# Output projection behind the whole gate, as seven products, with y turned by a DRAM trip and VectorE's 32x32 blocks

## The chip, the cores and the metric

The kernel runs on one NeuronCore of one Trainium2 chip. The metric is the device time of one execution in microseconds (us). Times before are given for three runs; one further execution was taken by the profiler, and every row of a profile in this document is of that execution.

## What is computed

The reference is a transformer block of two layers on one sequence of S = 2048 rows with D = 640 columns, in float32. The first layer is windowed attention, the second a gated MLP whose gate mixes rows:

```python
h  = x + attention(layernorm(x), wqkv, wo)       # 32 heads, window 256
z  = gelu(layernorm(h) @ w_in)                   # F = 1728
z1, z2 = z[..., :864], layernorm(z[..., 864:])
g  = w_sp @ z2 + b_sp[:, None]                   # w_sp is 2048 x 2048
h2 = h + (z1 * g) @ w_out                        # w_out is 864 x 640
```

Below, y is z1 * g, of 2048 x 864. Matrix products run on TensorE (PE) in three terms: each operand is split into a rounded high part and a remainder (fp32r), and hi·hi, hi·lo and lo·hi are summed in PSUM. A "piece" is such a pair hi, lo.

## The kernel before

The 2048 rows are 16 tiles of 128 (P). The stages follow each other: attention; residual and layer norm; z by pairs of tiles; then the gate g in two halves of w_sp's columns. The first gate (c = 0) takes the columns that meet the first eight tiles of z2 and stores partial sums to DRAM (g_d); the second gate (c = 1) takes the others, adds g_d's rows, then b_sp, and multiplies by z1.

The gate already goes by seven products instead of eight: tiles p and p + 8 of rows form a pair, w_sp's block and z2's columns are cut into 2x2 blocks, and B11, T1, T2, B22, T3, B21, T4 are blocks, or sums and differences of blocks, whose seven products give the four results (Strassen's scheme in Winograd's form). The pieces of w_sp lie in seven places of the buffer `aw`; the raw w_sp lies in `fx`, which has two halves of 2048 columns, one for each parity of the pair; z2's pieces are `zc` (tiles `ze`, `zl`). A gate pair is 7 x 4 x 3 = 84 matmuls of 128x432. Results are gathered in `rows[0]` to `rows[3]` (432 columns to each half).

In the second gate, the output projection of a pair of tiles is done inside the gate of the next pair. `turn_y` transposes a tile of y (128x864) on PE in seven pieces into PSUM, and ACT and VectorE (DVE) split it into `y_sp`. `final` multiplies it by w_out (`project`: 7 K tiles of 128, the last with 96 rows, 3 terms, 2 halves of 320 columns: 42 matmuls of 128x320 per tile), adds h, and stores the result. `h` rows are `hr` and `rows[1]`; w_out's pieces are `wout`. After the last gate pair, tile 14 and tile 15 of this sequence (banks `out_ps` and `out_l`) are left.

The program is a list, `steps`: one entry for each product with a post (the sum that reads the product's PSUM bank), and `at(n, f)` hangs f ahead of step n. In this part of the program no order is written out by hand: the tile scheduler takes the instructions with the list as its priority, works with modelled times, and sets the order of every engine's queue, SP's (SyncE, which issues the DMAs) among them. A queue is worked off in order, so a DMA that waits holds back all that stand behind it on SP. Dependencies become semaphore waits.

PSUM banks of the gate and the projection have tags "a" and "b" with four buffers each. `split`, `plus`, `minus` and `copy` are helpers: L717 is the line of all elementwise sums and differences (on DVE unless an engine is given), L723 that of ACT's copies.

The lines below are the functions that the change touches, with their line numbers in the profile.

Of the kernel before, what the change touches and what calls it, by code (L numbers as in the profile page):

```python
# [34 lines left out]
def block_kernel(ctx, tc, x, wqk, wv, wo, w_in, wsp, bsp, w_out, out):  # L35
# [99 lines left out]
    def split(hi, lo, raw, eng=None):  # L135

        nc.scalar.activation(hi, raw, AF.Copy)  # L137
        (eng or nc.vector).tensor_tensor(out=lo, in0=raw, in1=hi.bitcast(F32), op=OP.subtract)
# [571 lines left out]
    def bank(tag, name):  # L710
        if "d" not in pools:
            psK.close()
            pools["d"] = pool(ctx, "psD", space=PSUM)
        return pools["d"].tile([P, 512], F32, tag=tag, bufs=4, name=name)

    def plus(out, a, b, op=OP.add, eng=None):
        (eng or nc.vector).tensor_tensor(out=out, in0=a, in1=b, op=op)  # L717

    def minus(out, a, b, eng=None):
        plus(out, a, b, OP.subtract, eng)  # L720
# [41 lines left out]
    def two(t):  # L762
        return t[:, 0], t[:, 1]
# [75 lines left out]
    def open_e1():  # L839
        win_stack.close()  # L840
        p = pool(win_stack, "e1")
        e1["wout"] = p.tile([P, 2, KF, D], F32R, name="wout")
        e1["y"] = p.tile([P, 2, KF, P], F32R, name="y_sp")
        e1["z1"] = [p.tile([P, FH], F32, name=f"z1_{n}") for n in range(2)]
        e1["h"] = [p.tile([P, D], F32, name="hr"), rows[1][:, :D]]

    def turn_h(i):
        ht = mem["ho"][i % 3]
# [14 lines left out]
    def at(n, f):  # L863
        later.setdefault(n, []).append(f)
# [210 lines left out]
    def gate_pair(p, c, post, extra):  # L1075
# [81 lines left out]
        def prod(m, half, start, stop, ks=range(4)):  # L1157
            if (m in (B11, T1) or m == B21 and alone) and ks[0] == 0:
                gbank[key(m, half)] = bank("b" if m == B21 else "a", f"g{c}_{p}_{half}_{m}")
            ps = gbank[key(m, half)][:, :HF]  # L1160
            for k in ks:
                if c == 1 and p == 7 and m == T4 and k == 2:
                    turn_y(NT - 2, e1["y"])
                for x, y in ((0, 0), (0, 1), (1, 0)):
                    nc.tensor.matmul(ps, w[m][x][:, k], zc[k][m][:, y], start=start and k + x + y == 0,  # L1165
                                     stop=stop and k == 3 and x == 1, skip_group_check=True)
# [27 lines left out]
                                            (plus, g11), (copy, g21))], lambda m: None)  # L1194


    y_sp2 = view(aw, 0, 2, KF, P)

    def turn_y(n, dst, tag="b"):
        y = e1["z1"][n % 2]  # L1200
        for k0, k1 in ((0, 4), (4, KF)):
            ps = bank(tag, f"yt_ps{n}_{k0}")
            for k in range(k0, k1):
                w = min(P, FH - k * P)
                nc.tensor.transpose(ps[:w, (k - k0) * P:(k - k0 + 1) * P], y[:, k * P:k * P + w], ident)
            for k0, k1, w in ((0, 4, P),) if k0 == 0 else ((4, 6, P), (6, 7, FH - 6 * P)):
                o = (k0 % 4) * P
                split(dst[:w, 0, k0:k1], dst[:w, 1, k0:k1],
                      ps[:w, o:o + (k1 - k0) * P].rearrange("p (k t) -> p k t", k=k1 - k0))

    def project(ps, js, src, middle=None):
        for k in range(KF):
            if k == 3 and middle is not None:
                middle()
            w = min(P, FH - k * P)
            for a, b in ((0, 0), (0, 1), (1, 0)):
                for j in js:
                    nc.tensor.matmul(ps[j][:, :HD], src[:w, a, k, :], e1["wout"][:w, b, k, j * HD:(j + 1) * HD],  # L1218
                                     start=(k == 0 and a + b == 0), stop=(k == KF - 1 and a == 1))

    def tile_of(n):
        return n // 2 + 8 * (n % 2)

    def load_h(n):
        nc.sync.dma_start(e1["h"][n % 2], h_d[tile_of(n)])

    def final(n, middle=None):
        ps = [bank("b", f"out_ps{n}_{j}") for j in range(2)]
        project(ps, range(2), e1["y"], middle)
        for j in range(2):  # L1230
            final_half(ps, n, j, j == 1)

    def final_half(ps, n, j, store):
        ht, c = e1["h"][n % 2], slice(j * HD, (j + 1) * HD)
        plus(ht[:, c], ps[j][:, :HD], ht[:, c])
        c = slice(0 if store == 1 else j * HD, (j + 1) * HD)
        if store:
            nc.sync.dma_start(out[tile_of(n) * P:(tile_of(n) + 1) * P, c], ht[:, c])

    gate_rows = (rows[n] for n in [0, 1] + [2, 0, 3] * 5)  # L1240

    def second_gate(p):
        i, j = 2 * p, 2 * p + 1
        gi, gj = next(gate_rows), next(gate_rows)
        n0 = len(steps)
        if p == 0:
            at(n0, open_e1)
        g = {11: gi[:, :HF], 12: gi[:, HF:], 21: gj[:, :HF], 22: gj[:, HF:]}

        def add(n):  # L1250
            def run(ps):
                plus(g[n], ps, g[n])
                side["tick"] = g[n][:, :1]
            return run

        def gated(n):
            t, c = (p + 8, j) if n > 20 else (p, i)
            z = e1["z1"][c % 2][:, HF * (n % 10 - 1):HF * (n % 10)]
            nc.vector.scalar_tensor_tensor(out=z, in0=g[n], scalar=bcol[:, t:t + 1], in1=z, op0=OP.add, op1=OP.mult)

        def load_z(n):
            nc.sync.dma_start(e1["z1"][n % 2], z1_d[tile_of(n)])

        turns = (0, 1, 2, 3) if p > 1 else (0, 4, 4, 6)

        def extra(m):
            if p:
                for x, f in zip(turns, (lambda: turn_y(i - 2, e1["y"]), lambda: final(i - 2),
                                        lambda: turn_y(i - 1, e1["y"]), lambda: final(i - 1))):
                    if x == m:  # L1270
                        f()

        at(n0 - (0 if p else 1), lambda: nc.sync.dma_start(gi, g_d[p]))
        at(n0, lambda: nc.sync.dma_start(gj, g_d[p + 8]))
        at(n0 + (1 if p else 0), lambda: load_z(i))
        at(n0 + (turns[2] + 1 if p else 0), lambda: load_z(j))
        at(n0 + 4, lambda: gated(12))
        at(n0 + (6 if p == 1 else 5), lambda: gated(22))
        at(n0 + 6, lambda: gated(11))
        at(n0 + 7, lambda: gated(21))  # L1280
        at(n0 + (9 if p == 0 else 6), lambda: load_h(i))
        at(n0 + (11 if p == 0 else 7), lambda: load_h(j))
        gate_pair(p, 1, [add(11), add(22), add(12), add(12), add(22), add(11), add(21)], extra)
        if p == 0:
            def wout_raw(k):
                if k < 3:
                    return view(fx, 2048 + k * D, D)
                return e1["h"][0] if k % 2 else rows[3][:, :D]

            def load_wout(k):  # L1290
                nc.sync.dma_start(wout_raw(k), w_out[k * P:(k + 1) * P, :])

            def put_wout(k):
                one = const.tile([P, 1], F32, tag="onew", bufs=2, name=f"onew{k}")
                nc.vector.tensor_scalar(out=one, in0=side["tick"], scalar1=1.0, scalar2=1.0, op0=OP.max, op1=OP.min)
                hi, lo = (e1["wout"][:, t, k] for t in range(2))
                nc.scalar.activation(hi, wout_raw(k), AF.Copy, scale=one)
                minus(lo, wout_raw(k), hi.bitcast(F32))

            for k, (t, u) in enumerate(((-9, 1), (-8, 2), (-7, 3), (0, 4), (2, 6), (4, 8), (6, 9))):  # L1300
                at(n0 + t, lambda k=k: load_wout(k))
                at(n0 + u, lambda k=k: put_wout(k))

    for p in range(8):
        z_pair(p, 2 * p, 2 * p + 1, win1)
# [7 lines left out]
        z2_pair(12 + p, p + 8, p + 12, p)  # L1313
    for p in range(8):
        second_gate(p)

    def run(n):
        for f in later.pop(n, []):
# [51 lines left out]
        if n > 2:  # L1370
            next(w2p, None)
    run(len(steps))
    run(len(steps) + 1)
    assert not later, sorted(later)
    n = NT - 2
    final(n, lambda: turn_y(n + 1, y_sp2, "a"))
    ps = [bank("b", f"out_l{j}") for j in range(2)]
    for j in range(2):
        project(ps, (j,), y_sp2)
        final_half(ps, n + 1, j, 2)  # L1380


# [25 lines left out]
```

## Time and profile before

| | |
|---|---|
| runs | 1109.02, 1111.28, 1111.66 us; median 1111.28 us |
| profiled execution, first to last instruction (span) | 1108.2 us |
| PE busy | 1084.3 us, 98% |
| VectorE (DVE) busy | 720.7 us, 65% |
| ScalarE (ACT) busy | 571.0 us, 52% |
| GpSimd (POOL) busy | 369.6 us, 33% |
| DMA | 187.80 MB, mean 169 GB/s |

The page gives no other time for the profiled execution than its span; the three runs lie 0.8 to 3.5 us above it, the median 3.1 us. Stages in the span: the second gate with the projections from 861.4 us to about 1090, the last two tiles to 1104.8 us, and the last stores to the end. In a row of groups, `xN` is the number of instructions, then come the sum of their busy time in us and the mean of one in ns, then the engine's idle time ahead of them. "PEld" is the loading of matmul weights, which lies beside PE's work. In a row of windows the columns are PE, PEld, DVE, ACT and POOL busy with the instructions of each, then the clock granted to PE, the share of the 16 DMA engines' time that was taken, and the GB/s moved.

### The profile page before, as it was taken

To read this page: it belongs to the slowest core of one execution; us is meant where nothing else is said; L and a number is where in the kernel's file an instruction comes from. 1 tells how busy PE (TensorE), PEld (TensorE's weight loads), DVE (VectorE), ACT (ScalarE), POOL (GpSimd) and SP (SyncE) were. 2 spreads that over 40 slices of the span, in tenths; PEclk is the share of its full clock that TensorE was granted. 3 is DMA by queue.
4 is the path that set the end of the run, shared out by engine and by line. 5 is a ranking of instruction groups with operands and counts; after the bars stand their busy time and mean duration, and the time that the engine had idled before them with its cause. 6 is when DMAs were issued, how large, how long until landed. Compare 5 with 4: busy or idle time off the path is not lost.

```text
span 1108.2 us, 27795 instructions
## 1 busy us (share of the span) xinstructions
PE 1084.3 (98%) x10667; PEld 974.4 (88%) x10667; DVE 720.7 (65%) x2043; ACT 571.0 (52%) x1215; POOL 369.6 (33%) x524
## 2 busy tenths in 40 slices
PE   9999999999999999989999999999999999999998
PEld 7998877668888877788899999999999999999998
DVE  6541212879999998677567478676637985566543
ACT  4333433249999999567776567433326531122210
POOL 3114444457777778512100055256422000000000
PEclk9999999999999999999999999999999999999999
DMA  7212565565666654678755421447593663444321
GB/s 261 74 35 96 166 221 179 196 210 181 214 204 214 215 177 120 193 254 281 242 188 193 151 80 39 165 154 233 190 339 113 204 215 114 129 132 150 100 91 65
DMA packets 88501, 187.80 MB, mean 169 GB/s; under 512 B 11648, under 2 KB 48144, under 8 KB 84448
## 3 DMA queue, kind: packets, MB, share of 16 engines
q1 hardware_dynamic: 83728, 172.08, 47.8%
q0 software_dynamic: 2336, 8.70, 2.2%
q10 hardware_dynamic: 2304, 5.24, 1.2%
q8 instruction: 84, 1.38, 0.5%
q14 instruction: 49, 0.40, 0.1%
HBM read 121.66 MB, written 65.52 MB: 169 GB/s over the span
## 4 chain that ended last, share of the span: by engine, by line
PE 78%; DMA 8%; DVE 3%; issue 3%; POOL 3%; ACT 3%; SPq 2%; ACTq 0%; POOLq 0%; DVEq 0%
PE g L1165 20%; PE zb L968 9%; PE out_ps L1218 8%; PE pv L435 6%; PE bank L341 5%; PE bank L407 5%; PE zx L916 3%; PE zv L916 2%; PE qk L525 2%; PE qk L526 2%; PE qk L527 2%; DMA qk_d<-sg 2%; PE zy L916 2%; SPq L320 1%; PE zw L916 1%
## 5 line engine op out<-in xcount | busy, mean ns | idle before, releaser
L410 ACT ACTIVATE pt<-bank 128x384 f32<-128x384 f32 (+2 forms) x512 | 200.8, 496 | 10.4 <-PE bank L407 5.7
L1165 PE MATMUL g<-zl,aw 128*128 128x432 f32 x768 | 169.7, 359 | 0.0
L353 DVE CUSTOM_DVE_ANT_0 junk<-bank,strip 128x288 bf16<-128x288 f32 x392 | 157.7, 454 | 4.3 <-PE bank L341 3.0
L723 ACT ACTIVATE aw<-fx 128x512 fp32r<-128x512 f32 (+2 forms) x147 | 84.9, 592 | 141.1 <-PE g L1165 101.9
L1165 PEld LDWEIGHTS g<-zl,aw 128*128 128x128 f32 x768 | 143.5, 188 | 6.1
L1165 PE MATMUL g<-ze,aw 128*128 128x432 f32 x576 | 131.9, 359 | 1.1 <-DVE row L717 1.1
L435 PE MATMUL pv<-pt,v_sb 128*32 128x192 f32 (+3 forms) x1984 | 127.3, 323 | 3.8 <-POOL pt L415 1.3
L717 DVE TENSOR_TENSOR aw<-fx,aw 128x512 fp32r<-128x512 f32 (+2 forms) x146 | 99.4, 690 | 28.6 <-ACT aw L723 23.5
L1165 PEld LDWEIGHTS g<-ze,aw 128*128 128x128 f32 x576 | 107.1, 188 | 6.2 <-DVE row L717 1.8
L407 PE MATMUL bank<-slot 123*32 123x288 bf16 (+5 forms) x1536 | 106.1, 282 | 1.0 <-ACT pt L410 0.4
L412 POOL TENSOR_SCALAR_AFFINE_SELECT pt<-pt 128x512 f32<-128x512 f32 x128 | 82.9, 648 | 43.6 <-ACT pt L410 42.4
L1218 PE MATMUL out_ps<-wout,y_sp 128*128 128x320 f32 (+1 forms) x630 | 96.4, 309 | 0.4 <-ACT y_sp L137 0.4
L968 PE MATMUL zb<-win,aw 128*128 128x432 f32 x480 | 95.0, 359 | 0.5 <-ACT aw L723 0.5
L1218 PEld LDWEIGHTS out_ps<-wout,y_sp 128*128 128x128 f32 (+1 forms) x630 | 94.2, 188 | 1.0 <-ACT y_sp L137 0.7
L968 PEld LDWEIGHTS zb<-win,aw 128*128 128x128 f32 x480 | 90.1, 188 | 5.0 <-ACT aw L723 0.9
L341 PE MATMUL bank<-slot 120*32 120x288 bf16 (+2 forms) x1264 | 89.8, 285 | 1.1 <-DVE mcol L353 1.0
L541 DVE TENSOR_TENSOR rest<-qk,sg 128x512 f32<-128x512 f32 x40 | 27.7, 692 | 86.1 <-ACT sg L539 86.1
L415 POOL TENSOR_SCALAR_AFFINE_SELECT pt<-pt 128x512 f32<-128x512 f32 x112 | 74.6, 666 | 0.0
L717 DVE TENSOR_TENSOR row<-g,row 128x432 f32<-128x432 f32 x80 | 48.2, 603 | 33.8 <-PE g L1165 30.3
L544 POOL TENSOR_TENSOR sg<-rest,sg 128x512 bf16<-128x512 f32 x40 | 46.6, 1166 | 69.2 <-ACT sg L543 60.2
L435 PEld LDWEIGHTS pv<-pt,v_sb 128*32 128x32 f32 x1984 | 59.5, 110 | 10.3 <-POOL pt L415 3.2
L407 PEld LDWEIGHTS <-slot 123*32 123x32 bf16 x1536 | 52.6, 96 | 16.2 <-issue 5.0
(216 smaller groups left out, 2195.1 us busy)
## 6 DMA issues: line engine op xcount, KB each, us to landing
fx<-wsp_in SPq DMA_DIRECT2D x30, 512.0 KB
slot<-qk_d SPq DMA_DIRECT2D x72, 200.0 KB
qk_d<-sg SPq DMA_DIRECT2D x32, 384.0 KB
slot<-qk_d SPq DMA_DIRECT2D x72, 160.0 KB
fx<-hn_d SPq DMA_DIRECT2D x32, 320.0 KB
o_d<-ot SPq DMA_DIRECT2D x64, 128.0 KB
z_d<-row SPq DMA_DIRECT2D x18, 432.0 KB
g_d<-row SPq DMA_DIRECT2D x16, 432.0 KB
```

The source lines that it names most:

```text
L341: nc.tensor.matmul(ps[32 * j:32 * j + 32, :n], part(st, half, 120, 0, hh, q0, 32), part(st, half, 120, 1, hh, lo + skip * j, n), start=Tru ...
L353: nc.vector.tensor_tensor_reduce(out=junk[:, :n], in0=ps[:, :n], in1=keep, scale=1.0, scalar=NEG, op0=OP.add, op1=OP.max, accum_out=m_cols ...
L407: nc.tensor.matmul(ps[32 * i:32 * i + 32, b:e], part(st, half, 123, 1, hh, k0, 32), part(st, half, 123, 0, hh, kb * P + b, e - b), start=T ...
L410: nc.scalar.activation(pt[:, hh, :n], ps[:, :n], AF.Exp, scale=SCALE)
L412: nc.gpsimd.affine_select(out=pt[:, :, :P], in_=pt[:, :, :P], pattern=[[0, 4], [1, P]], base=0, channel_multiplier=-1, compare_op=OP.is_ge ...
L435: nc.tensor.matmul(ps[32 * hh:32 * hh + 32, a - 512 * c:b - 512 * c], v_sb[:, kb, v0:v0 + 32], pt[:, hh, a - kb * P:b - kb * P], start=fir ...
L717: (eng or nc.vector).tensor_tensor(out=out, in0=a, in1=b, op=op)
L723: nc.scalar.activation(out, a, AF.Copy)
L916: nc.tensor.matmul(ps, a[x], b[:, y], start=start and m + x + y == 0, stop=stop and m == n - 1 and x == 1, skip_group_check=True)
L968: nc.tensor.matmul(b[0][:, :HF], a[t][:, x, kk], win2[0][:, y, kk, h * HF:(h + 1) * HF], start=kk + x + y == 0, stop=kk == KD - 1 and x == 1)
L1165: nc.tensor.matmul(ps, w[m][x][:, k], zc[k][m][:, y], start=start and k + x + y == 0, stop=stop and k == 3 and x == 1, skip_group_check=True)
L1218: nc.tensor.matmul(ps[j][:, :HD], src[:w, a, k, :], e1["wout"][:w, b, k, j * HD:(j + 1) * HD], start=(k == 0 and a + b == 0), stop=(k == K ...
```

## The change

The second gate no longer contains the projection. Its eight pairs follow each other, 84 matmuls each, and y's tiles are stored to a DRAM buffer. Then come eight `out_pair`s, which are one product of 2x2 blocks each: rows are tiles n and n + 8, columns are w_out's two halves of 320, and K is cut into two halves of 3 tiles. Seven products of 3 K tiles (63 matmuls) do the work of 6 K tiles, and K tile 6 (96 rows) is multiplied in the plain way for the four results (12 matmuls). That is 75 matmuls of 128x320 per pair, 600 in all, in place of 672.

y gets its transposed form so: `store_y` writes a tile to `y_d` by four DMAs, each of 32x27 runs of 32 floats, such that block columns come to lie as wanted; `load_y` reads a tile back by two DMAs, one of 96 partitions x 896 whose DRAM side is 3 x 32 x 896, one of 32 x 768; and `turn_y` is now one VectorE transposition of 32x32 blocks of 128x896. w_out's rows are put in an order to match, outside of the kernel. The sums of y's blocks (`y_prep`) are made on GpSimd, their high parts on ACT, their low parts on VectorE and two of eight on GpSimd. w_out's pieces go into z2's places `zc` as these come free in the last gate pair; its sums are made on GpSimd in gate pairs 2 to 5. Each out pair has nine sums into h's rows of 128x320 by VectorE, and one row of h and one of the result per tile, as before.

The core of the diff:

```diff
+    y_d = dram.tile([NT, 32, 4 * KF * P], F32, name="y_d")
...
-                if c == 1 and p == 7 and m == T4 and k == 2:
-                    turn_y(NT - 2, e1["y"])
...
-    def turn_y(n, dst, tag="b"):
...
-    def project(ps, js, src, middle=None):
...
-    def final(n, middle=None):
...
+        def store_y(t):
+            dst = y_d[(i, j)[t]].rearrange("j (c a i) -> a j c i", a=4, i=32)
+            for a in range(4):
+                nc.sync.dma_start(dst[a, :, :FH // 32],
+                                  y(t)[32 * a:32 * a + 32, :FH].rearrange("j (c i) -> j c i", i=32))
...
+    def y_block(n, t):
+        return view(fx, (n + 1) % 2 * 2048 + t * KF * P, KF * P)
+
+    def load_y(n, t):
+        y, src = y_block(n, t), y_d[n + 8 * t].rearrange("j (b c) -> b j c", b=4)
+        nc.sync.dma_start(y[:96], src[:3])
+        nc.sync.dma_start(y[96:, :6 * P], src[3, :, :6 * P])
+
+    def turn_y(n, t, k0, k1):
+        nc.vector.transpose(e1["yt"][t][:, k0 * P:k1 * P], y_block(n, t)[:, k0 * P:k1 * P])
...
+        return [(-4, lambda: (plus(a("s1"), a(21), a(22), eng=pool), hi(B11, a(11)))),
+                (-3, lambda: (hi(T1, a("s1")), lo(B11, a(11)), minus(a(21), a(11), a(21), pool))),
+                (-2 if n else -1, lambda: hi(B21, whole(0))),
+                (-2, lambda: (lo(T1, a("s1")), minus(a(11), a("s1"), a(11), pool))),
+                (-1, lambda: (hi(T2, a(11)), lo(B21, whole(0)), minus(a(12), a(12), a(11), pool))),
+                (0, lambda: (hi(B22, a(12)), lo(T2, a(11)), hi(T3, a(21)))),
+                (1, lambda: (lo(B22, a(12)), lo(T3, a(21), pool), hi(T4, whole(1)))),
+                (2, lambda: lo(T4, whole(1), pool))]
...
+        steps.extend([
+            (lambda: prod("v", T1, True, False), lambda: plus(c22, ps("v"), c22)),
+            (lambda: prod("x", B11, True, False), lambda: plus(c11, ps("x"), c11)),
+            (lambda: prod("y", B21, True, True, 0), lambda: plus(c11, ps("y"), c11)),
+            (lambda: prod("x", T2, False, False), lambda: plus(c12, ps("x"), c12)),
+            (lambda: prod("v", B22, False, True, 1), lambda: plus(c12, ps("v"), c12)),
+            (lambda: prod("x", T3, False, True), post5),
+            (lambda: (prod("z", None, True, True, 3, False), prod("w", T4, True, True, 2)), post6)])
```

PE's queue in the second gate, gate pairs 4 and 5 before: gate matmuls (`g1_4` and `g1_5` are the pairs' banks), the turning of a tile of y (`yt_ps`) and projections (`out_ps`) in one stream.

```order
L1205 MATMUL yt_ps6_0_14034<-ident_76,z1_0_13110 128x128 x4
L1205 MATMUL yt_ps6_4_14041<-ident_76,z1_0_13110 128x128 x2
L1205 MATMUL yt_ps6_4_14041<-ident_76,z1_0_13110 96x128
L1165 MATMUL g1_4_0_0_14021<-ze2_10530,aw_9622 128x432 x3
L1165 MATMUL g1_4_0_0_14021<-ze9_10537,aw_9622 128x432 x3
L1165 MATMUL g1_4_0_0_14021<-zl4_9605,aw_9622 128x432 x3
L1165 MATMUL g1_4_0_0_14021<-zl11_9612,aw_9622 128x432 x3
L1165 MATMUL g1_5_0_0_14268<-ze0_10528,aw_9622 128x432 x3
L1165 MATMUL g1_5_0_0_14268<-ze7_10535,aw_9622 128x432 x3
L1165 MATMUL g1_5_0_0_14268<-zl2_9603,aw_9622 128x432 x3
L1218 MATMUL out_ps6_0_14067<-wout_13108,y_sp_13109 128x320
L1218 MATMUL out_ps6_1_14068<-wout_13108,y_sp_13109 128x320
```

The same queue now, gate pairs 3 and 4:

```order
L1166 MATMUL g1_3_1_1_13540<-ze3_10532,aw_9623 128x432 x3
L1166 MATMUL g1_3_1_1_13540<-ze10_10539,aw_9623 128x432 x3
L1166 MATMUL g1_3_1_1_13540<-zl5_9607,aw_9623 128x432 x3
L1166 MATMUL g1_3_1_1_13540<-zl12_9614,aw_9623 128x432 x3
L1166 MATMUL g1_3_0_0_13519<-ze6_10535,aw_9623 128x432 x3
L1166 MATMUL g1_3_0_0_13519<-zl1_9603,aw_9623 128x432 x3
L1166 MATMUL g1_3_0_0_13519<-zl8_9610,aw_9623 128x432 x3
L1166 MATMUL g1_3_0_0_13519<-zl15_9617,aw_9623 128x432 x3
L1166 MATMUL g1_4_0_0_13651<-ze2_10531,aw_9623 128x432 x3
```

Only gate matmuls are left there; the turnings are gone from PE and the projections stand behind the last gate pair.

SP's queue in the second gate before, about one gate pair of it (`z1_0` and `z1_1` are z1's two buffers, `row` are g_d's rows or h's, `fx` takes the raw w_sp):

```order
L1262 DMA z1_0_13110<-z1_d_69 128x864 [waits DMAHW2_49,PE_49]
L1273 DMA row3_9620<-g_d_71 128x864 [waits DVE_49]
L1262 DMA z1_1_13111<-z1_d_69 128x864 [waits DMAHW4_49,PE_49]
L1238 DMA h2_out<-hr_13112 128x640 [waits DVE_49]
L1225 DMA hr_13112<-h_d_68 128x640 [waits DMAHW6_49,DMAHW5_49]
L1238 DMA h2_out<-row1_9618 128x640 [waits DMAHW7_49,DVE_49]
L1225 DMA row1_9618<-h_d_68 128x640 [waits DMAHW7_49,DMAHW0_49]
L1274 DMA row2_9619<-g_d_71 128x864 [waits DMAHW1_49,DVE_49]
L1091 DMA fx_9623<-wsp_in 128x1024 [waits DMAHW2_49,DVE_49]
```

The same now, one gate pair (`y2` and `y3` are two of y's four buffers, which take z1 first):

```order
L1231 DMA y_d_72<-y3_13115 32x27x32 [waits DMAHW5_49,DVE_49]
L1231 DMA y_d_72<-y3_13115 32x27x32 x3
L1223 DMA row3_9621<-g_d_71 128x864
L1231 DMA y_d_72<-y2_13114 32x27x32 [waits DMAHW2_49,DVE_49]
L1231 DMA y_d_72<-y2_13114 32x27x32 [waits DMAHW3_49]
L1231 DMA y_d_72<-y2_13114 32x27x32 [waits DMAHW4_49]
L1231 DMA y_d_72<-y2_13114 32x27x32 [waits DMAHW5_49]
L1223 DMA row2_9620<-g_d_71 128x864 [waits DMAHW6_49]
L1226 DMA y3_13115<-z1_d_69 128x864 [waits DMAHW7_49,DMAHW0_49]
L1094 DMA fx_9624<-wsp_in 128x1024 [waits DVE_49]
L1226 DMA y2_13114<-z1_d_69 128x864 [waits DMAHW4_49,DMAHW3_49,DMAHW5_49,DMAHW2_49,DMAHW1_49]
L1094 DMA fx_9624<-wsp_in 128x1024 [waits DVE_49]
```

Eight stores of y have come in and the four rows of h and of the result have gone out. The loads of z1 wait for the landing of the stores from the same buffer, and the loads of the raw w_sp stand behind them.

SP's queue where the gate ends and the out pairs begin (`fx<-y_d` is `load_y`, here of out pair 1; `row<-h_d` is a row of h):

```order
L1297 DMA fx_9624<-y_d_72 96x1x896 [waits DMAHW6_49,DMAHW1_49,DVE_49]
L1298 DMA fx_9624<-y_d_72 32x768 [waits DMAHW2_49]
L1231 DMA y_d_72<-y1_13113 32x27x32 [waits DVE_49]
L1231 DMA y_d_72<-y1_13113 32x27x32 x2
L1231 DMA y_d_72<-y1_13113 32x27x32 [waits DMAHW3_49]
L1339 DMA row1_9619<-h_d_68 128x640 [waits DMAHW4_49]
```

The first loads of y, for out pairs 0 and 1, stand ahead of the stores of y of gate pairs 6 and 7, those for pairs 2 and 3 among the stores of gate pair 7.

More of the change, by code (lines that the diff above doesn't have):

```diff
@@ L1194, in first_gate @@
                                             (plus, g11), (copy, g21))], lambda m: None)
[L1197 to L1240 removed]
+    LAST = 7 * P
     def second_gate(p):
[L1243 to L1244 removed]
+        i, j = p, p + 8
+        gi, gj = (rows[(2 * p + t) % 4] for t in range(2))
         n0 = len(steps)
@@ L1252, in run, with y @@
                 plus(g[n], ps, g[n])
-                side["tick"] = g[n][:, :1]
             return run
+        def y(t):
+            return e1["y"][(2 * p + t) % 4]
         def gated(n):
[L1257 to L1262, printed above, removed]
```

159 lines of the change are left out of this document (118 added, 41 removed).

## The prediction

> **What bounds the kernel now.** I read the busy shares first, then windows over the last 250 us, then the chain that ended last, and behind these the groups, waits and queues of that stretch.
>
> ```profile
> PE 1084.3 (98%) x10667; PEld 974.4 (88%) x10667; DVE 720.7 (65%) x2043; ACT 571.0 (52%) x1215; POOL 369.6 (33%) x524
> 861.40:1090.00 228.60, 228.60 (x1359) 222.70 (x1358) 137.11 (x262) 57.35 (x108) 0.96 (x2) 1.00 0.44 141
> 1090.00:1104.80 14.80, 14.33 (x99) 13.80 (x97) 5.11 (x12) 2.18 (x6) 0.00 (x0) 1.00 0.18 56
> ```
>
> The second line is the second gate with the projections inside it. PE is busy in all of its 228.60 us at a granted clock of 1.00, VectorE in 60% of them, the DMA engines in 44%. PE alone bounds this stretch: a matmul that goes there shortens the kernel by its full time, as long as nothing else becomes late. The chain tells what PE does:
>
> ```profile
> 905.64 6.17 PE out_ps L1218 x42
> 911.81 0.77 PE yt_ps L1205 x7
> 912.58 4.12 PE g L1165 x21
> ...
> 1090.62 0.02 issue
> 1090.64 0.02 ACTq L137
> 1090.65 0.04 issue
> 1090.70 0.60 ACT y_sp L137
> 1091.30 0.04 issue
> 1091.35 0.86 PE out_ps L1218 x4
> ...
> 1104.78 0.49 DVE row L717
> ```
>
> A projection matmul takes 6.17/42 = 0.147 us, a gate matmul 4.12/21 = 0.196, a transposition 0.77/7 = 0.110. PE's one wait there, 1090.62 to 1091.35, is the split of the last tiles' y: 0.7 us.
>
> **The change part by part: PE.** The counts before:
>
> ```profile
> L1218 PE MATMUL out_ps<-wout,y_sp x630: 302/309/417, 888.0 to 1098.3; 128*128 128x320 f32 x135, 96*128 96x320 f32 x23
> L1218 PE MATMUL out_l<-wout,aw x42: 302/310/314, 1098.4 to 1104.4; 128*128 128x320 f32 x36, 96*128 96x320 f32 x6
> L1205 PE MATMUL yt_ps<-ident,z x112: 270/272/273, 877.8 to 1092.7; 128*128 128x128 f32 x96, 128*96 128x128 f32 x16
> ```
>
> 672 projection matmuls become 600 of the same shape: 72 x 0.147 = 10.6 us less. 112 transpositions go: 112 x 0.110 = 12.3. The wait in the tail goes: 0.7. Together 23.6 us off the path. PE alone would now need 8 x 84 x 0.196 = 131.7 us for the gate (16.46 per pair) and 600 x 0.147 = 88.2 for the out pairs (75 x 0.147 = 11.0 each).
>
> **The tail.** Before, one sum of 0.49 us follows the last matmul. Now four stand there, since two products have two readers each. Three more at 0.44 (6.2/14, the group `row<-out_ps` below) are +1.3 us.
>
> **The gate pairs without cover.** The groups of VectorE and GpSimd:
>
> ```profile
> L717 DVE TENSOR_TENSOR row<-g,row 128x432 f32<-128x432 f32 x56 | 33.8, 603 | 15.2 <-PE g L1165 11.7 <-DMA row<-g_d 3.3
> L717 DVE TENSOR_TENSOR aw<-fx,aw 128x512 fp32r<-128x512 f32 x42 | 28.5, 682 | 0.7 <-ACT aw L723 0.7
> L1259 DVE SCALAR_TENSOR_TENSOR z<-row,bcol,z 128x432 f32<-128x432 f32 x32 | 21.2, 664 | 1.5 <-DMA z<-z_d 1.3
> L717 DVE TENSOR_TENSOR row<-out_ps,row 128x320 f32<-128x320 f32 x14 | 6.2, 486 | 33.3 <-PE out_ps L1218 33.3
> L138 DVE TENSOR_TENSOR y_sp<-yt_ps,y_sp 128x256 fp32r<-128x256 f32 x15 | 6.2, 415 | 0.0
> L717 DVE TENSOR_TENSOR wout<-fx,wout 128x640 fp32r<-128x640 f32 x3 | 2.4, 816 | 0.0
> L717 POOL TENSOR_TENSOR side_parts<-side_raw,side_parts 128x432 fp32r<-128x432 f32 x7 | 8.4, 1197 | 0.1
> L717 POOL TENSOR_TENSOR side_parts<-side_raw,side_parts 128x512 fp32r<-128x512 f32 x6 | 8.1, 1343 | 0.5
> ```
>
> Per gate pair VectorE has 7 posts x 0.603, 4 gatings x 0.664, and for w_sp 7 low parts and 4 sums at 0.682: 14.4 us of PE's 16.46, 87%, where the projection used to stretch the pair to 30 us. I take +1 us of stalls over the eight pairs; 0 to 8 is the range, the upper end being one 128x512 per pair and a half on the path. The work on w_out's pieces (GpSimd's sums, 9 low parts of 128x320 on VectorE) moves from the first pair to pairs 2 to 7 and costs nothing: GpSimd is idle in the gate (0.96 us in the window above), and VectorE's 9 x 0.44 = 4 us lie where pair 7's own w_sp work thins out. If that cover is gone, up to 4 us wait at the first out pair.
>
> **The trip of y through DRAM, storing.** The queue before, and windows that give prices:
>
> ```profile
> fx<-wsp_in SPq DMA_DIRECT2D x12, 512.0 KB
> z<-z_d SPq DMA_DIRECT2D x16, 432.0 KB
> row<-g_d SPq DMA_DIRECT2D x15, 432.0 KB
> SPq L1262 <- PE yt_ps L1205: 65.1, 13, 11.3
> DVE tmp L717 <- DMA fx<-wsp_in: 7.4, 3, 2.5
> 807.20:823.70 16.50, 16.50 (x86) 15.81 (x85) 6.25 (x10) 3.91 (x7) 5.50 (x8) 1.00 0.91 324
> 923.40:954.30 30.90, 30.90 (x188) 30.13 (x186) 17.28 (x33) 6.60 (x13) 0.00 (x0) 1.00 0.43 135
> 246.20:246.60 0.40, 0.40 (x12) 0.32 (x8) 0.00 (x0) 0.15 (x1) 0.40 (x2) 0.50 0.20 45
> ```
>
> In large rows one DMA engine moves 324/(0.91 x 16) = 22.3 bytes per ns, in the second gate 135/(0.43 x 16) = 19.6. A gate pair loads 2 x (512 + 432 + 432) KB, 176 kB per engine: 7.9 us at 22.3. The new stores are 2 x 3456 runs of 128 bytes, 432 per engine. In the last window only `slot<-mt` moves, in rows of 256 bytes: 45/(0.20 x 16) = 14.1 bytes per ns, 18.2 ns a row. A run of 128 bytes costs between half of that and all of it, 9.1 to 18.2 ns; with no reason for either I take the middle, 13.6: 5.9 us. Sum 13.8 of 16.46 us: hidden, but SP used to wait 65.1 us for the turnings and now waits for these stores to land ahead of each z1 load, with w_sp's load behind it, and VectorE has waited for w_sp already (7.4 us in 3 waits). The point from which it decides is (16.46 - 7.9)/432 = 19.8 ns per run.
>
> The Trainium skill, "DMA: Bandwidth & Descriptors", Specifications, gives 512 bytes as the smallest transfer at line rate and says that smaller ones become read-modify-writes. No row here shows a 128-byte run alone; by that rule I would raise the price above the middle, and past 19.8 ns the second rival below holds.
>
> **Loading y back.** The large load of a tile has 3 x 32 x 896 on its DRAM side and 96 partitions on the other. The nearest case is that `slot<-mt`: 96 partitions on one side, 3 (rows 120 to 122 of `slot`) on the other.
>
> ```profile
> L373 DVE CAST mt<-bank x16: 281/285/291, 226.6 to 434.0; 120x128 bf16<-120x128 f32 x8, 96x128 bf16<-96x128 f32 x8
> 244.57 0.80 SPq L375 DMA_DIRECT2D slot<-mt  x1
> 245.42 4.20 SPq L320 DMA_DIRECT2D xb<-qk_d  x5
> 246.90:247.65 0.75, 0.75 (x20) 0.55 (x12) 0.73 (x4) 0.69 (x2) 0.00 (x0) 0.50 0.61 137
> ```
>
> While it ran alone (246.20 to 246.60) the DMA share was 0.20, that is 3.2 engines of 16. In the window just quoted only `xb<-qk_d` moves, whose outer count in the code is 20, at 0.61: 9.8 engines. So a transfer whose outer count is 3 runs on three engines here, and I take that for the load. Each of them gets 32 rows of 3584 bytes, 114.7 kB: 5.14 us per tile at 22.3, 10.3 per pair. The same three carry their sixteenth of the rest: the 32 x 768 loads 0.55, h 1.84 and the result 1.84 per pair. That is 14.5 us per pair against PE's 11.0: in the out pairs these three engines are the bound, not PE.
>
> The Trainium skill, same page, "Why a DMA increments its semaphore by 16 and not by 1", has the rule: the largest number up to 16 that divides the slowest dimensions of both sides. The trace agrees (3 rows 0.20, 20 rows 0.61).
>
> How much is late at the end: from the issue of the first load to the landing of the last, the three engines carry 8 x 10.85 of y, six pairs of h and four of results (10 x 1.84), one z1 load 1.2, and the last 864 runs of stores (11.8): 118.2 us. By SP's order the first load stands behind the stores of gate pair 5, whose last post I put 3 us behind that pair, and four issues of 0.8: 2 x 16.46 - 6 = 27 us ahead of the gate's end. The second load waits for `fx`, 1.5 us. The last load lands at 118.2 + 1.5 - 27 = 92.7 us after the gate. Then two transpositions, GpSimd's first sum (384 columns: 1.07), ACT's high part and VectorE's low part: 4.4 us. So the last pair starts at 97.1, where PE alone would start it at 7 x 11.0 = 77.1: 20 us late. At 19.6 bytes per ns the loads take 14.7 us more (35 late); the run price moves it by 4 each way; if the loads are spread over all engines, 0. I take 20, by the window nearest in row size.
>
> VectorE and GpSimd lie below that. VectorE per out pair: 9 sums x 0.486, 4 low parts of 384 columns at 0.55 (between 415 and 682 ns), one of 512 at 0.68, two transpositions. No row has one; by 816 ns for 640 columns, 896 take 1.14 us, by a slower path twice that. Together 9.6 to 11.8 us. GpSimd: five of 384 columns and one of 512, 5 x 1.07 + 1.34 = 6.7. Both are under 14.5, so they cost only their place in the last chain.
>
> **The sum.** 1108.2 - 23.6 + 1.3 + 1 + 20 = 1106.9 us of span. The median of the runs was 3.1 above the span, so 1110.0.
>
> **The rivals.**
> *Faster: the loads don't bind.* If the large loads use 16 engines, or their three engines move clearly more than 22.3 bytes per ns with the others idle, the out pairs run at PE's pace and only a start of about 2 us shows: 1108.2 - 23.6 + 1.3 + 1 + 2 + 3.1 = 1092. For it: the load's other side has 96 partitions, and no large load with an outer count of 3 is in the trace. Against it: the share of 0.20.
> *Slower: the stores of 128-byte runs pace the gate.* It decides from 19.8 ns per run. At 27 ns (1.5 times the 256-byte row's 18.2) a pair takes 432 x 27 = 11.7 + 7.9 = 19.6 us instead of 16.46, over seven pairs +22: 1132. For it: the in-order wait on SP and the price that no row shows. Against it: half the bytes of a 256-byte row.
> A change that does nothing is excluded, since PE's queue shows the turnings gone and 600 projections.
>
> One cost is left out of all:
>
> ```profile
> 242.26 0.29 PE L341 MATMUL bank<-slot 120*32 120x256 bf16 x4 [0.98 <-DVE mcol L353]
> 242.96 0.31 PE L407 MATMUL bank<-slot 123*32 123x288 bf16 x4 [0.41 <-ACT pt L410]
> 244.70:248.10 3.40, 3.40 (x61) 2.37 (x56) 2.34 (x12) 2.62 (x7) 1.91 (x5) 0.50 0.58 183
> ```
>
> After these two waits of PE its clock was 0.50 for 3.4 us. PE would now wait some 3 us per out pair. At half clock for 3.4 us a pair takes 11.0 + 1.7 = 12.7 us, still below 14.5, so it shows only once, at the end (+1.7).
>
> **How the numbers follow.** Three engines bind: 0.60, 1110, from 1098 (the y loads faster by a tenth) to 1125 (19.6 bytes per ns), which gives 0.24 faster, 0.18 same, 0.18 slower. Loads don't bind: 0.20, all faster. Stores pace the gate: 0.20, of it 0.03 same. The three runs spread by 0.24%, so 0.3% (3.3 us) is about what can be told from no change. Faster 0.44, same 0.21, slower 0.35. The range 1090 to 1128 takes in the first rival and leaves out most of the second.
>
> **What would show it.** Right: PE solid in the gate at 16.5 us per pair; in the out pairs PE busy near 75%, its waits ending in VectorE's transposition or a low part, these in `fx<-y_d`; a DMA share near 0.2 to 0.3 there; a landing time of the large load near 10 us. Wrong: out pairs of 11 to 12 us (the loads don't bind), or gate pairs of 18 us or more with PE waiting for w_sp's pieces.

## The result: slower, and the profile after

The changed kernel takes 1152.78 us (median of 4 runs, 1152.58 to 1153.92) against 1110.57 us for the kernel before (4 runs, 1109.02 to 1111.66). The ratio is 1.0378, with a 95% interval of 1.0352 to 1.0404: 42 us slower. The forecast was 1110 with a range of 1090 to 1128. The span of the changed kernel in the profile is 1152.2 us, 44.0 more than before.

The first rows of the changed kernel's profile; the two rows of digits cut the span into 40 slices and give PE's busy share and its granted clock in tenths:

```profile
PE 1078.5 (94%) x10483; PEld 963.7 (84%) x10483; DVE 772.7 (67%) x2086; ACT 586.9 (51%) x1239; POOL 457.6 (40%) x598
PE   9999999999999998989999999999999988578878
PEclk9999999999999999999999999999999999888979
```

PE is busy for less time than before (1078.5 us against 1084.3) and no longer fills the end: from slice 34 on it waits, and its clock is lowered there. Windows of the changed kernel cut the end into three parts, 624 of PE's gate matmuls, the junction from these to the out pairs, and the out pairs (the other 48 matmuls of the last gate pair stand among them):

```profile
861.60:996.80 135.20, 125.95 (x625) 115.72 (x623) 98.22 (x164) 36.91 (x64) 22.23 (x19) 1.00 0.78 209
996.80:1009.40 12.60, 0.95 (x3) 0.50 (x2) 8.77 (x12) 3.69 (x8) 3.52 (x3) 0.58 0.26 91
1009.40:1147.30 137.90, 112.41 (x646) 109.93 (x646) 86.55 (x138) 34.02 (x66) 61.96 (x54) 0.86 0.45 127
```

By the matmul times of before, the first part needs 624 x 0.196 = 122.3 us, so 12.9 are lost. The junction loses 12.3 (12.6 less two projection matmuls). The third part needs 598 x 0.147 + 48 x 0.196 = 97.3 us, so 40.6 are lost: 25.5 in waits (137.9 - 112.4) and 15.1 in matmuls at a lower clock (112.4 - 97.3). Together 65.8; less the 23.6 us that PE no longer does, and 1.5 more behind the last matmul, that is 43.7 of the 44.0.

What PE waits for is in the chain of the changed kernel:

```profile
989.65 0.73 SPq L1297
990.42 11.78 DMA fx<-y_d
1002.30 1.11 DVE yt L1301
...
1019.89 11.17 DMA fx<-y_d
...
1083.34 3.91 DMA h_out<-row
1087.75 0.71 SPq L1297
1089.06 11.03 DMA h_out<-row
1100.47 0.69 SPq L1297
1101.75 7.65 DMA h_out<-row
1109.42 6.25 DMA row<-h_d
```

A load of y takes 11 to 12 us to land where two follow each other. Behind the second such load the chain does not run through loads of y any more, but through results and rows of h: a store of a result, 11.03 us; another, 7.65; a row of h, 6.25. These are transfers of 320 KB and 128 rows; before the change, rows of that kind reached a DMA share of 0.91 (the prediction's window 807.20 to 823.70), so they are not bound to three engines. The waits of PE and VectorE (DVE) say the same; after the name of the releaser come the sum in us, the number of waits and the longest:

```profile
PE out_v L1357 <- DVE row L718: 12.0, 3, 7.0
PE out_y L1357 <- DVE aw L718: 10.7, 2, 5.7
DVE row L718 <- DMA row<-h_d: 28.4, 5, 9.5
```

About half of PE's 25.5 us of waits in the out pairs end in sums, and VectorE's sums waited 28.4 us for rows of h. Two windows in which little else than loads of y is under way, and SP's waits:

```profile
995.00:998.80 3.80, 1.85 (x10) 1.43 (x8) 1.11 (x2) 0.00 (x0) 0.00 (x0) 1.00 0.19 76
1092.00:1098.00 6.00, 2.84 (x12) 2.60 (x11) 3.12 (x7) 0.24 (x1) 0.72 (x1) 0.71 0.19 74
SPq L1339 <- DMA h_out<-row: 52.3, 10, 10.6
SPq L1369 <- DVE row L718: 30.4, 8, 6.0
```

A share of 0.19 is three engines of 16, each at 76/(0.19 x 16) = 25 bytes per ns. A result's share on these three stands behind the loads, and only its landing frees the row for the next h. SP waits 52.3 us for such landings, in order, with the next loads of y behind. That the loads on three engines are what makes the landings late is what the experiments test.

### The profile page after: what moved, and what is told of

Same layout as the page of the kernel before. It is cut to its first block, busy times and chain, and to the rows that moved or that the text cites. A ratio compares the mean times of both kernels' runs of the same rounds, so it can differ in the third digit from the quotient of the medians.

```text
span 1152.2 us, 27727 instructions
## 1 busy us (share of the span) xinstructions
PE 1078.5 (94%) x10483; PEld 963.7 (84%) x10483; DVE 772.7 (67%) x2086; ACT 586.9 (51%) x1239; POOL 457.6 (40%) x598
## 3 DMA queue, kind: packets, MB, share of 16 engines
q8 instruction: 82, 1.34, 0.5%
## 4 chain that ended last, share of the span: by engine, by line
PE 60%; DMA 16%; DVE 8%; SPq 6%; issue 4%; ACT 3%; POOL 3%; DVEq 0%; ACTq 0%; POOLq 0%
PE g L1166 12%; PE zb L971 8%; PE pv L436 6%; PE bank L408 5%; PE bank L342 5%; DMA h_out<-row 3%; PE zx L919 2%; SPq L1231 2%; DVE aw L718 2%; PE zv L919 2%; DMA fx<-y_d 2%; PE qk L526 2%; PE qk L528 2%; PE qk L527 2%; DMA row<-h_d 2%
## 5 line engine op out<-in xcount | busy, mean ns | idle before, releaser
L718 DVE TENSOR_TENSOR aw<-fx,aw 128x512 fp32r<-128x512 f32 (+2 forms) x146 | 103.4, 718 | 29.8 <-ACT aw L724 24.6
L724 ACT ACTIVATE aw<-yt 128x384 fp32r<-128x384 f32 (+1 forms) x48 | 26.0, 557 | 85.8 <-DVE yt L1301 29.0
L354 DVE CUSTOM_DVE_ANT_0 junk<-bank,mask 128x384 bf16<-128x384 f32 (+2 forms) x120 | 50.8, 449 | 15.1 <-PE bank L346 12.3
```

The source lines that it names most:

```text
L354: nc.vector.tensor_tensor_reduce(out=junk[:, :n], in0=ps[:, :n], in1=keep, scale=1.0, scalar=NEG, op0=OP.add, op1=OP.max, accum_out=m_cols ...
L724: nc.scalar.activation(out, a, AF.Copy)
```

## The experiments

Theory A: the loads of y run on three engines, and what else these carry is late with them. Theory B: four buffers for the rows of h make SP wait for landed results. Theory C: the stores in 128-byte runs pace the gate. Theory D: VectorE's own queue is what is late.

Each run's ratio is to executions of the kernel before that were made beside it, whose medians lie between 1110.17 and 1113.03 us. The executions of one kernel also differ by several us ahead of the change: in the profiled ones the first matmul of the second gate starts between 857.95 and 868.89 us, and the first gate's first matmul already has this spread (688.69 to 699.79). So the stretch from the second gate's first matmul to the end is given too, "from the gate on". It is 246.9 us before the change and 290.7 after it, of one execution each.

**Split loads**

```diff
-        nc.sync.dma_start(y[:96], src[:3])
+        for b in range(3):
+            nc.sync.dma_start(y[32 * b:32 * b + 32], src[b])
```

> Only the large load of y is changed: three DMAs of 32 partitions in place of one of 3 x 32. Theory A (three DMA engines carry the loads, so a load lands after 10 to 12 us, and results and h queue behind it there): a load lands in 3 to 5 us, the out stage falls from 138 us to about 105, PE's clock there comes back to 1.00, time about 1115 us. Theory B (h's rows have four buffers, so each load of h waits for the landing of a result, and SP, in order, holds the loads of y behind that wait): most of SP's 52 us of waits stay, the out stage stays above 125 us, time about 1140 us.

Measured: 1115.16 us, ratio to before 1.0019 (0.9987 to 1.0051). This one edit takes back 37.6 us by the medians, 40 by the ratios, 41 from the gate on (249.7). The windows and SP's wait in this run:

```profile
996.80:1009.40 12.60, 7.76 (x35) 7.01 (x34) 11.89 (x17) 3.70 (x8) 3.52 (x3) 0.86 0.68 156
1009.40:1103.00 93.60, 91.28 (x592) 88.56 (x591) 83.97 (x127) 33.82 (x66) 64.41 (x54) 1.00 0.61 173
SPq L1340 <- DMA h_out<-row: 20.3, 10, 3.4
```

PE is busy in 91.28 of 93.60 us of the out pairs at clock 1.00, the longest wait for a result fell from 10.6 to 3.4 us, and VectorE's waits for rows of h from 28.4 to 4.0 us. The out pairs are at PE's pace now, with the same bytes and with four buffers as before. A is what made them slow.

**Two engines in place of three**

```diff
-        nc.sync.dma_start(y[:96], src[:3])
+        nc.sync.dma_start(y[:64], src[:2])
+        nc.sync.dma_start(y[64:96], src[2])
```

> Only the large load of y: two DMAs, one of 64 partitions (outer count 2 on the DRAM side), one of 32 (outer count 32), in place of one of 3 x 32. If the outer count sets the number of engines, the 64 partitions run on two engines with 32 rows each: the same 114.7 kB per engine as before, the same 10 to 12 us to landing, and a time within 8 us of the changed kernel's 1153 us. If instead the bytes in one DMA or the number of DMAs is what counts, a third of the way to the split loads' 1115 us: about 1140 us or less.

Measured: 1158.85 us, 1.0412 (1.0389 to 1.0434). A third of the rows left the slow transfer, and the kernel became no faster (293.7 us from the gate on, 3 more than the changed kernel). A window of this run in which little else than loads of y is under way:

```profile
997.00:1001.00 4.00, 1.09 (x6) 0.69 (x4) 1.43 (x2) 0.22 (x1) 0.00 (x0) 0.94 0.13 50
```

A share of 0.13 is two engines of 16, again at 25 bytes per ns each. So it isn't the number of DMAs or the bytes in one, but the rows per engine, which the outer count sets.

**Eight buffers for the rows of h**

```diff
-        h = [rows[(2 * n + t) % 4][:, :D] for t in range(2)]
+        def hb(t):
+            return (rows + e1["y"])[(2 * n + t) % 8][:, :D]
```

> Only the rows of h and the result are changed: eight buffers in place of four (y's four buffers are free by then), so a load of h waits for a result of four pairs before. Theory A (three engines): the loads still need 14.5 us per pair on their three engines, out stage 125 to 135 us, time 1140 to 1150 us. Theory B (SP waits for the results' landing): SP's 52 us of waits go, out stage 105 to 115 us, time about 1125 us.

Measured: 1141.03 us, 1.0269 (1.0151 to 1.0387): 11.8 us less than the changed kernel by the medians, 13.9 from the gate on (276.8). The interval, of two runs, still reaches the changed kernel's ratio, and the time lies at the low end of what theory A alone gave. SP's waits did not go; where a buffer comes round again they are as long as before, and VectorE now waits for loads of y (6.7 us in the out pairs before this edit) in place of rows of h:

```profile
SPq L1345 <- DMA h_out<-y: 29.8, 4, 11.9
SPq L1345 <- DMA h_out<-row: 19.7, 4, 11.8
DVE yt L1301 <- DMA fx<-y_d: 17.8, 3, 6.7
DVE row L718 <- DMA row<-h_d: 4.6, 2, 3.6
```

So B costs some 12 to 14 us, the smaller part of the loss, and behind it stand the loads on three engines.

**Both edits**

> Both edits: the split loads and eight buffers for h. If A and B are both at work, the out stage comes to 95 to 100 us and the time to about 1108 us. If A alone is, it equals the run with split loads within 4 us. If neither, VectorE and GpSimd chains hold the out pairs at 15 us or more and the time stays above 1135 us.

Measured: 1113.74 us, 1.0008 (0.9976 to 1.0039), within 1.5 us of the split loads alone (247.7 us from the gate on, 2.0 less). The expectation for A alone, within 4 us, held. With short loads the buffers' reuse costs next to nothing: B was a consequence of A.

**Stores in long runs**

```diff
-            dst = y_d[(i, j)[t]].rearrange("j (c a i) -> a j c i", a=4, i=32)
+            dst = y_d[(i, j)[t]][:, :4 * FH].rearrange("j (a c) -> a j c", a=4)
             for a in range(4):
-                nc.sync.dma_start(dst[a, :, :FH // 32], ...)
+                nc.sync.dma_start(dst[a], y(t)[32 * a:32 * a + 32, :FH])
```

> Only the stores of y are changed: the same bytes in four DMAs per tile, but in runs of 3456 bytes in place of 128 (y_d's order is then not the one that the loads assume; the loads move the same bytes as before). If the 128-byte runs pace the gate (by engine time and by SP waiting for their landing), the gate falls from 135 us for its 624 matmuls to about 125, the wait between gate and out pairs from 12 us to 5, time about 1135 us. If VectorE at 87% paces it, gate and time stay within 4 us of 1153 us.

Measured: 1150.65 us, 1.0355 (1.0232 to 1.0479). This kernel leaves out the order in which y must come to lie, so its result is not the block's; only its time is of use. PE's waits ahead of the gate's matmuls, first in the changed kernel, then in this run:

```profile
L1166 PE MATMUL g<-ze,aw 128*128 128x432 f32 x288 | 68.0, 364 | 11.0 <-DVE row L718 6.0 <-DVE aw L718 4.6 <-ACT aw L724 0.2
```

```profile
L1166 PE MATMUL g<-ze,aw 128*128 128x432 f32 x288 | 67.8, 366 | 4.7 <-DVE row L718 3.5 <-DVE aw L718 0.7 <-ACT aw L724 0.4
```

The waits fell by 6.3 us, and the gate's first 624 matmuls took 129.5 us in place of 135.4: about half of the 10 us that C was to give. The median fell by 2 us only, where 18 were expected, but in the profiled execution the gate began 3.5 us later than in the changed kernel's; from the gate on it took 282.3 us, 8.4 less. The waits of the junction stayed (9.02 and 3.42 us ahead of the first product's two halves, 8.24 and 3.42 before). So C costs some 6 us in the gate, of one execution each.

**PE kept warm**

```diff
             ps = banks[name][:, :HD]
+            if name == "v" and start:
+                for _ in range(16):
+                    nc.tensor.matmul(ps, wout(B11, 0)[:, 0, :P], wout(B11, 0)[:, 0], start=True, stop=True, ...)
```

> The changed kernel with 16 matmuls of 128x320 more ahead of each out pair's first product (into a bank that this product then overwrites): 128 x 0.147 = 18.8 us of PE work that no result needs. The out stage lost 25 us to PE's waits and 15 us to its clock of 0.50. If the loads set the pace and the clock's loss lies in what would be waits anyway, the time stays within 5 us of 1153 us. If the half clock is itself on the path, PE now stays warm and the time falls by 5 to 12 us. If PE's work bounds the out stage, the time rises by up to 19 us.

Measured: 1156.14 us, 1.0387 (1.0328 to 1.0447), of two runs, 1150.80 and 1161.48 us. 18.8 us of PE work more cost 3 us by the medians, between 2 us less and 9 more by the two runs, and the clock in the out stage rose from 0.86 to 0.91:

```profile
1009.40:1155.00 145.60, 122.53 (x762) 120.12 (x761) 87.86 (x142) 34.27 (x66) 58.85 (x54) 0.91 0.42 121
```

By the same count as above (762 matmuls, 48 of them the gate's) the lower clock costs 8.2 us here in place of 15.1, and the time did not fall for it. Neither PE's work nor its clock set the pace of the out pairs. The 15.1 us at the lower clock lay in time that would have been waits.

**Another layout of y in DRAM**

```diff
         def store_y(t):
+            nc.sync.dma_start(y_d[(i, j)[t]], y(t)[:, :FH])
...
     def load_y(n, t):
+        y = y_block(n, t).rearrange("p (a f) -> p a f", a=4)
+        src = y_d[n + 8 * t].rearrange("(a j) f -> j a f", a=4)
+        for b in range(4):
+            f = min(7 * 32, FH - 7 * 32 * b)
+            nc.sync.dma_start(y[32 * b:32 * b + 32, :, :f], src[:, :, 7 * 32 * b:7 * 32 * b + f])
...
+        nc.vector.transpose(e1["yt"][t].rearrange("p (c a j) -> p a c j", a=4, j=32),
+                            y_block(n, t).rearrange("p (a c i) -> p a c i", a=4, i=32))
```

> The trip of y in another layout: a tile is stored by one DMA of 128 x 864 (rows of 3456 bytes), loaded by four DMAs of 32 partitions x 4 runs of 896 bytes, and the transposition writes its 32x32 blocks in the order that the store no longer makes. Theory (three engines was the cause, 128-byte runs and SP's eight issues a smaller one): beside the gain of the split loads (1115 us) the gate's waits of PE fall by the 5 to 7 us that the run with long runs showed: about 1108 us. Rival (what is left is VectorE's queue in the gate): 1113 to 1116 us.

Measured: 1107.26 us, 0.9973 (0.9946 to 1.0000). Against the split loads the ratio fell by 0.0046, 5 us, though the two intervals overlap a little; from the gate on it fell by 7.2 us, to 242.5. PE's waits ahead of the gate's matmuls fell from 9.6 to 6.0 us, those ahead of `out_v`'s from 5.3 to 2.8. So C's cost shows with A away; since this edit changes the loads too, the 5 to 7 us are not all shown to be the stores'. No store has a run under 3456 bytes now, no load under 768.

With eight buffers for h as well:

> The layout of the run before and eight buffers for the rows of h. With loads of y short, the reuse of h's buffers should be hidden: within 3 us of the run with the layout alone. If the reuse still held SP back, 4 us or more less.

Measured: 1106.72 us, 0.9994 (0.9966 to 1.0021), 244.0 us from the gate on. No difference that can be told, as expected.

**Six buffers for the rows of g_d**

```diff
-        gi, gj = (rows[(2 * p + t) % 4] for t in range(2))
+        def grow(t):
+            return (rows + [x[:, :FH] for x in e1.get("yt", [])])[(2 * p + t) % 6]
```

> The same and six buffers for g_d's rows in the second gate in place of four (the two buffers of transposed y serve as rows 4 and 5 until the out pairs), so a load of g_d no longer waits for the gating of the pair before the last. Theory (PE's waits in the gate end in VectorE's posts, which wait some 19 us in all for loads of g_d): these waits go, PE's idle time in the gate falls from about 9 us to 3, time 4 to 6 us below the run with eight h buffers. Rival (VectorE, busy 87% in the gate, is late by its own work): no change beyond 2 us.

Measured: 1108.84 us, 0.9963 (0.9939 to 0.9987). The median did not fall, but the ratio did, and the intervals overlap. In the traces VectorE's waits for rows of g_d in the gate are gone (7.4 us in the run with eight h buffers), and from the gate on it took 238.8 us in place of 244.0; but PE's waits in the gate did not fall, they end in ACT's high parts in part, and the granted clock of the other execution was lower (0.97 in the gate, 1.00 here). So this run neither shows the theory nor excludes it. D isn't shown either: in the run with the new layout alone the chain that ended last spends 26.3% of the gate in landings of the raw w_sp, for whose loads SP waited 28.1 us until VectorE had freed the halves of `fx`. More room for the raw w_sp was not tried.

**All of w_out's low parts on GpSimd**

```diff
-            minus(lo, wout_block(m)[:, k], hi.bitcast(F32), nc.gpsimd if m in (T1, B22, T3, B21) else nc.vector)
+            minus(lo, wout_block(m)[:, k], hi.bitcast(F32), nc.gpsimd)
```

> The kernel with the new layout and eight buffers for h, and all of w_out's low parts on GpSimd (9 of 128x320 leave VectorE). Between the gate's last pair and the first out pair VectorE is busy over 90% and PE waits some 7 us for its sums and low parts. Theory (VectorE is late there): 4 us less on VectorE, 3 to 5 us below the 1106.7 us of the run without this edit. Rival (GpSimd, with 23 low parts of about 1 us in one pair, becomes late itself, or slows VectorE as much): no change or up to 4 us more.

Measured: 1106.94 us, 0.9946 (0.9916 to 0.9976). The median is that of the run without the edit; the ratio is lower by 0.0048, and the intervals overlap. From the gate on it took 238.1 us in place of 244.0, with the same difference of clock as in the run before (the same kernel took 240.6 in the next profile). Inconclusive on D.

The same kernel once more, with more executions:

> The kernel with the new layout, eight buffers for h and w_out's low parts on GpSimd again, against the kernel before in five rounds. From the three rounds it had (ratio 0.9946, 0.9916 to 0.9976): 0.993 to 0.997, faster than before by 3 to 8 us. PE's work alone would give 1092 us; if what is left is waits at the junction of gate and out pairs, the time stays some 12 us above that.

Measured: 1106.02 us against 1111.58 for the kernel before, 0.9954 (0.9930 to 0.9977). The new layout, with eight buffers for h and w_out's low parts on GpSimd, makes the change a gain of some 5 us, 0.5%; which of the three gives how much of it is open beyond what stands above. Its windows:

```profile
861.60:996.80 135.20, 128.98 (x649) 120.99 (x648) 107.27 (x177) 42.24 (x76) 28.32 (x24) 1.00 0.67 221
996.80:1009.40 12.60, 10.71 (x50) 9.36 (x49) 11.58 (x15) 5.61 (x14) 10.06 (x9) 0.86 0.61 190
1009.40:1103.00 93.60, 92.17 (x609) 90.17 (x607) 79.92 (x124) 31.12 (x59) 61.46 (x54) 1.00 0.53 161
```

PE is busy in 128.98 and 10.71 us of the first two windows, where it was in 125.95 and 0.95, and in 98% of the third, where it was in 82%. The time still lies 14 us above the 1092 that PE's work alone would give. PE is idle for 9.5 us in the three windows, 8.1 of them ahead of 1009 us.

## Why the prediction was wrong, point by point

**What bounds the kernel, and PE's share: right.** The removal of 23.6 us from PE closes the account above to 0.3 us, at 0.147 us per projection matmul where the clock is 1.00.

**The tail: right.** From the last matmul to the end it takes 3.4 us before and 4.9 after: 1.5 more, against 1.3 forecast. (The three sums at their row's own mean of 486 ns, in place of 6.2/14 = 0.44, are 1.46.)

**Three engines: right.** The share of 0.19, the split loads and the share of 0.13 in the run on two engines show it; with the loads split, the share was 0.79 between 999 and 1001 us, where loads of y were under way. The Trainium skill's rule ("DMA: Bandwidth & Descriptors", "Why a DMA increments its semaphore by 16 and not by 1") agrees with all three: 3, 16 and 2 engines by the outer count. The rate was 25 bytes per ns, better than the 22.3 that I took.

**The lateness of the out pairs: the step that failed.** The prediction added up the bytes of the three engines, 14.5 us per pair, as if these engines were never idle, and came to 20 us. The out pairs lost 40.6 and the junction 12.3. What the sum left out is the round trip: in the chain of the changed kernel results land 4 to 11 us after their issue, since they queue behind loads on these engines; only then is the row of h loaded, 6 to 8 us more; and SP, in order, has the next load of y behind that wait. A pair took (137.9 - 48 x 0.196)/8 = 16 us, where the three engines' bytes at 25 bytes per ns need 14.5 x 22.3/25 = 13 (an estimate), so the engines were idle for part of each pair. The prediction gave that wait no term at all, though it named SP's order for the gate. Eight buffers (12 to 14 us less, VectorE's waits for rows of h 28.4 to 4.6 us) and the split loads (SP's longest wait 10.6 to 3.4 us) show it. With eight buffers the out pairs still lose 30 us where 20 were forecast (132.1 us from 1007.47 us, behind the junction, to the end, less 97.3 of PE's work and 4.9 of the tail); the last 10 are not taken apart.

**The start of the out pairs: failed too.** I let the first load's landing be free, since it would be issued 27 us ahead of the gate's end. It was issued at 988.35 us, 18 ahead of that end (8.5 for the matmuls up to 996.85, 9.4 for the other 48). And the first product of out pair 0 stands in PE's queue ahead of 48 matmuls of the last gate pair, and PE works in order:

```profile
1005.09 0.90 PE L1357 MATMUL out_v<-ze,aw 128*128 128x320 f32 x2 [8.24 <-ACT aw L724]
1009.42 0.90 PE L1357 MATMUL out_v<-ze,aw 128*128 128x320 f32 x2 [3.42 <-DVE aw L718]
```

These two waits, 11.7 us, are the junction. They end in the loads of y for this pair: the second large one was issued at 989.65 us, and the last of the four landed at 990.42 + 11.78 = 1002.2. Transposition, sum, high part and low part follow. With split loads the same two waits were 1.07 and 3.77 us. The order of the changed kernel would have shown where that product stands.

**The gate: sized wrongly.** +1 us was taken with a range to 8; it lost 12.9. The end of most of PE's waits is VectorE's sums and low parts (6.0 and 4.6 of 11.0 us). The long runs take 6.3 of the waits away, so about half of the mis-sizing is the 128-byte stores, which the prediction had priced at 13.6 ns a run and called hidden. As throughput they were: a DMA share of 0.78 of the 18.2 us that a pair took is 14.2 us, against 13.8 added up. The waits come from SP's order, where the loads of g_d and of the raw w_sp stand behind eight stores: in the chain of the changed kernel's gate 15.0% is issuing stores of y and 11.3% landings of rows of g_d, in the run with long runs 3.0% and 3.3%. What makes the rest of the gate's waits is open. The Trainium skill's remark on transfers under 512 bytes ("DMA: Bandwidth & Descriptors", Specifications) pointed the right way, and its size here is 5 to 8 us. The second rival's pace, gate pairs at 19.6 us, did not come, but the sign named for it did, pairs of 18 us or more: they took 135.2/(624/84) = 18.2.

**The signs named beforehand.** PE was busy in 82% of the out pairs (75% named) and a large load landed in 11 to 12 us (10 named). But the DMA share was 0.45 there, not 0.2 to 0.3, and about half of PE's waits ended in sums that stood behind rows of h, not in the pieces of y. That is the same wait that the sum left out. A slower kernel had a chance of 0.35, through slower engines or the stores; the way it came about was not among the rivals.

**The clock: right in kind.** It fell to 0.50 behind PE's waits:

```profile
1000.00:1010.00 10.00, 1.49 (x4) 1.09 (x5) 7.70 (x11) 2.58 (x6) 3.52 (x3) 0.50 0.32 102
```

The loss of 15.1 us was many times the 1.7 that I had, but the run with more PE work shows that it was not on the path. The Trainium skill ("TensorE: Matmul & The Clock Gate", "HAM oscillation") has such falls behind idle gaps of more than about 3.4 us; the 8.24 us wait above is such a gap, but the clock fell about 2 us into it, earlier than that rule says (PE was idle from 996.85 us, and the mean granted clock was 0.63 between 998.80 and 999.20 and 0.50 behind).

**VectorE's transposition: right; its neighbours not.** The transposition, and two groups of the out pairs of the changed kernel:

```profile
L1301 DVE STREAM_TRANSPOSE yt<-fx x16: 1069/1101/1112, 997.7 to 1130.6; 128x896 f32<-128x896 f32 x16
L718 DVE TENSOR_TENSOR aw<-yt,aw 128x384 fp32r<-128x384 f32 x23 | 19.0, 826 | 2.2 <-ACT aw L724 2.2
L718 POOL TENSOR_TENSOR aw<-yt,aw 128x512 fp32r<-128x512 f32 x8 | 12.2, 1523 | 4.8 <-ACT aw L724 2.9 <-PE out_w L1357 1.7
```

The transposition took 1.10 us against 1.14 forecast. VectorE's low parts of 384 columns took 0.83 us, not 0.55, and GpSimd's of 512 columns 1.52 us, not 1.34.

## What to carry to other kernels

Before a transfer is called hidden, look at the outer dimension of both of its sides: a count of 3 puts it on three of 16 engines, and then everything else that these engines carry is late with it, the small transfers too. A sum of bytes per engine is only a lower bound on the time; where a buffer is used again after a store has landed, and the queue that issues the next load waits in order for that landing, add the round trip. And when a new stage is let into an engine's queue ahead of the rest of the old one, the first wait of the new stage stops both.

## What the runs showed of the hardware that was not expected

A 320 KB store of 128 rows, for which SP waited 3.4 us at most with split loads, took up to 11 us beside loads on three engines. VectorE's sums of two SBUF operands are slower beside GpSimd's work: those of 128x512 in the changed kernel's gate took 1.04 us on average between 880 and 890 us, where GpSimd was busy for 9.36 of 10 us, and 0.68 us between 890 and 975, where it was idle. In the out pairs, beside 62 us of GpSimd work, those of 384 columns took 0.83 us, where 0.55 was estimated from rows with GpSimd idle. A VectorE transposition of 32x32 blocks with a permuted output is one instruction and costs the same as the plain one:

```profile
L1300 DVE STREAM_TRANSPOSE yt<-fx x16: 1068/1099/1112, 992.7 to 1087.9; 128x896 f32<-128x896 f32 x16
```

The median is 1.10 us in the last kernel, as in the changed one.
